# Attention scores with the keys as the streamed operand: rows of scores are copied out and turned, where keys were the stationary operand and gave columns of scores

## The chip, the cores and the metric

One core of a Trainium2 chip runs the whole program in one launch. The metric is device time in microseconds, from start to end of one execution; three runs of the kernel before gave 1105.93, 1108.88 and 1117.53, so the median is 1108.88. Engines are named as the profile names them: PE (TensorE matmul) and PEld (its weight loads), DVE (VectorE), ACT (ScalarE), POOL (GpSimd), SP (the queue that issues the DMAs).

## The reference

Eight rows with one token each (D = 448) go through two layers with the same weights. Each layer is attention over a cache of 4096 keys and values, then a small MLP block. With one token per row the shifted concatenation in the block contributes nothing, because every shift moves the only token out of the sequence:

```python
def _A_ref(x, k_cache, v_cache, wq, wo):        # B=8, Hq=16, Hkv=8, Sk=4096, Dh=256
    q = (x @ wq).reshape(B, 1, Hq, Dh).transpose(0, 2, 1, 3)
    k, v = jnp.repeat(k_cache, 2, axis=1), jnp.repeat(v_cache, 2, axis=1)
    p = softmax(einsum("bhqd,bhkd->bhqk", q, k) * Dh ** -0.5)
    return einsum("bhqk,bhkd->bhqd", p, v).reshape(B, 1, 4096) @ wo

for _ in range(2):
    x = x + _A_ref(layernorm(x), k_cache, v_cache, wq, wo)
    y = layernorm(x)
    x = x + y + gelu(layernorm(y) @ w3) @ w4
```

Keys and values are bf16, 2 MB each for one head of one row (a head here is one of the 8 pairs of K and V, which serves two query heads). 64 such heads are read in each layer. Both layers read the same cache, so a part of it can stay on the chip between a row's first and second layer.

## The kernel before, in words

**Tiles and slots.** A head's K or V is cut into four units of 512 KB ("quarters"); the tile `kv` has 30 slots of one unit each. Position m of 128 partitions holds 32 consecutive keys, 8 of them in each unit. For a row's heads 3 to 7 (`kept_heads`) most of K, and the last 6 units of V, stay in their slots from the first layer to the second; heads 0 to 2 (`free_heads`) are loaded anew in both. A load is issued as soon as a slot is given free, by the scores for K (`o.frees` in `front`) and by the PV products for V (in `back`). Neighbouring units whose slots lie together go in one DMA of up to 2 MB.

**One head, first half (`front`).** Each new K unit arrives with keys along the partitions. `transpose_piece` turns it on PE in pieces: two bf16 elements are taken as one fp32, four 128x128 transposes (L1219) fill a bank `psT` (four banks), and DVE (L1202) or ACT (L1203) copies it back over the unit in `kv`. After it the 256 dimensions of a key lie on 128 partitions, the even and the odd ones in alternate elements (`c`, a step of two). The scores of a unit (`sc`, L1037) are 16 matmuls: for 8 groups of 128 keys and both `c`, the turned keys are the 128 stationary columns, and the two query columns, repeated `REP` = 24 times, are the 48 streamed columns. A score lands with its key on a partition, two columns per group, in `psM[:, 256 + 2i]`. From these 64 columns per head follow the softmax steps: copy to `sS` (L1056), maximum (L1059, over the partitions on POOL L1061), `nb` (L1065), exponentials to `pT` (ACT L1071), their sum (POOL L1075).

**One head, second half (`back`).** PV (L1104): for each group of 128 keys the two columns of `pT` are stationary and 256 columns of V are streamed; four groups of keys use four column groups of the array (`tile_position=(0, 32 * (i % 4))`), so that four partial sums stand on partitions 0, 32, 64 and 96. DVE copies and splits them into two bf16 parts (L1118, L1120), four small matmuls with `sel` add them (L1128), and L1134 divides. Four matmuls (L1153) add the head's share of `x @ wo` to a row in `psR`; when 7 heads are in, two DVE steps (L1163, L1165) and ten matmuls turn that row (`turn`), and the last head is added by L979 and L982.

**Order.** The functions do not emit instructions. They record operations with their engine, a duration in microseconds, what they read and write, the PSUM banks they use, and a priority; the class `Plan` then lays them out in time and writes one fixed order per engine, with semaphores between them. An operation of kind "ev" goes to DVE or ACT, whichever the planner finds free. An operation that touches a bank waits for the last user of that bank on each other engine. The planner also puts `filler` matmuls (L1424: 248 columns into a `psP` bank, or 512 into a `psT` bank) where it thinks PE is idle and the recent number of streamed columns is low, to keep PE's clock up.

**Loops.** Row by row: the kept heads of a row's first layer, the free heads of the next row drawn into them (`both`); then `mid` (MLP, L725 to L982, and the second layer's queries, L817 with L1275); then the second layer's heads, kept ones first; weights are loaded once (L605).

Of the kernel before, what the change touches and what calls it, by code (L numbers as in the profile page):

```python
# [6 lines left out]
P = 128  # L7
B = 8
D = 448
# [15 lines left out]
REP = 24  # L25
# [16 lines left out]
PV1 = PV0 + DH  # L42
QW, HW, YW = 24, 24, 12
SC = 448
YC = 0

# [414 lines left out]
def bass_interleave_layers__gqa_block_cached__mixer_s_mlp__decode_kernel(  # L461
# [53 lines left out]
    xoT = sb("xoT", [P, NC5, B - 2], bf)  # L515
    acc = [sb(f"acc{i}", [P, NC5], f32) for i in range(2)]
    base = sb("base", [P, NC5, B], f32)
    mask = sb("mask", [P, NC5], bf)
    xc = sb("xc", [P, NC5, B], f32)
    mom = sb("mom", [P, 3, B], f32)  # L520
# [5 lines left out]
    t_h = sb("t_h", [P, 28], f32)  # L526
    var = sb("var", [P, 2, B], f32)
    rsi = sb("rsi", [P, 2, B], i32)
    rst = sb("rst", [P, 2, B], f32)
    rsy = sb("rsy", [P, 2, B], f32)  # L530
    yb = sb("yb", [P, NC5, B], bf)
# [3 lines left out]
    o_last = sb("o_last", [P, G], bf)  # L535
    q2T = [sb(f"q2T{i}", [P, 32], bf) for i in range(2)]
    cursor[0] = (cursor[0] + 31) // 32 * 32
    hb0 = cursor[0]
    hb = sb("hb", [P, 14 * B], bf)
    g1 = sb("g1", [P, 14 * B], f32)  # L540
    row0 = cursor[0] - 448
    g2 = sb("g2", [P, 14 * B], f32)
    hT = sb("hT", [P, 14 * B], bf)

    oW = nc.alloc_sbuf_tensor_at("oW", [P, 2 * D], bf, offset=hb0)
    cursor[0] = max(cursor[0], hb0 + 4 * D)

    x_row = nc.alloc_sbuf_tensor_at("x_row", [B, NC5 * P], bf, offset=row0)
    o_row = nc.alloc_sbuf_tensor_at("o_row", [B, D], bf, offset=row0)
    assert row0 + 2 * NC5 * P <= hb0 + 4 * D  # L550
# [11 lines left out]
    oS = sb("oS", [P, 2, DH], bf)  # L562
    sel = sb("sel", [P, 2], bf)
# [10 lines left out]
    psM, M, SB = nc.alloc_psum_tensor("psM", [P, 512], f32), "M", 256  # L574
# [33 lines left out]
    def dma_once(name, parts, keys, at):  # L608

        for i, (dst, src, nbytes, *row) in enumerate(parts):  # L610
            dma(name, dst, src, nbytes, nc.alloc_semaphore(f"s_{name}{i}"), 16, [keys[i]],
                4 * at - 0.5, *row)
# [27 lines left out]
    YB = ["yb"]  # L640

    def const_a(gp):
        gp.memset(ident_f[:, :], 0.0)
        gp.memset(x_row[:, D:D + P], 0.0)
        gp.memset(mask[:, :], 1.0)
        gp.memset(x3T[:, :, :], 0.0)
        for t, c in [(t, 1) for t in x1c + x2c] + [(xf, 2)]:
            gp.memset(t[:, :, c:c + 1], 1.0)
            last = gp.memset(t[:, :, c + 1:c + 2], -1.0)
        return last  # L650
    plan.op("pool", const_a, 1.0, "const", wr=["ident0", "xr2", "mask0", "one", "x3all"])
# [48 lines left out]
    def rsqrt(c, n):  # L700
# [6 lines left out]
        for half, three in RSQRT_STEPS:  # L707
            dv(lambda v: v.tensor_tensor(tt, yy, yy, ALU.mult), rd=["rsy"], wr=["rst"])
            dv(lambda v, half=half: v.scalar_tensor_tensor(tt, tt, -half, vv, ALU.mult, ALU.mult),
               rd=["rst", "var", "var1"], wr=["rst"])  # L710
# [46 lines left out]
    def norm(src, skey, second, B):  # L757
# [23 lines left out]
        if second:  # L781
# [4 lines left out]
           rd=["mom", skey], wr=["xc"])  # L786
# [3 lines left out]
           rd=["xc", "rsy"], wr=["yb"])  # L790
# [72 lines left out]
    def last_rows(src, skey, n, ps, bank):  # L863
# [28 lines left out]
        def yrow(t):  # L892
            last = None
            for fc in range(14):
                for g in range(4):
# [7 lines left out]
                                            ALU.add), 0.2, rd=["psM", "xs"], wr=["o_last"], banks=[bank])  # L903
# [5 lines left out]
    def mlp(src, skey, n, dst, dkeys):  # L909
# [6 lines left out]
        h_, a_, b_ = hb[:, 0:m], g1[:, 0:m], g2[:, 0:m]  # L916
        if few:
# [4 lines left out]
            for r in range(n):  # L922
                dv(lambda v, r=r: v.tensor_scalar(t_h[:, r * 14:(r + 1) * 14], cs_h[:, :], minus_mean(n, r),
                                                  rsy[:, 1, r:r + 1], ALU.mult, ALU.mult),
                   rd=["mom", "rsy", "cs_h"], wr=["t_h"] if r == 0 else [("t_h", r)])
# [7 lines left out]
        else:  # L933
# [7 lines left out]
           rd=HB, wr=["g1"])  # L941
        dv(lambda v: v.scalar_tensor_tensor(b_, a_, GELU_K, h_, ALU.add, ALU.mult),
           rd=HB + ["g1"], wr=["g2"])
        plan.op("act", lambda a: a.activation(a_, b_, ACT.Tanh), 0.3, "chain",
                rd=["g2"], wr=["g1"], prio=urge[0] + len(plan.ops))
# [49 lines left out]
    def front(layer, b, h, prio=None):  # L995
# [8 lines left out]
        if layer == 0:  # L1004
            def rhs(c):
                return q1T[:, b, 4 * h + 2 * c:4 * h + 2 * c + 2]
            qk = [("q1T", 0), ("q1T", 1)]
        else:
            def rhs(c):
                return q2T[b % 2][:, 4 * h + 2 * c:4 * h + 2 * c + 2]  # L1010
            qk = [("q2", b, h)]
# [10 lines left out]
        for u in range(4):  # L1022
# [6 lines left out]
            def sc(t, u=u, q=ks[u]):  # L1029
                last = None  # L1030
                for s in range(8):
                    i = 8 * u + s


                    for c in range(2):
                        a = slot_ap(q, s * 256, 256)
                        last = t.matmul(ps[:, SB + 2 * i:SB + 2 * i + 2 * REP], a[:, c:256:2],  # L1037
                                        bcast(rhs(c), REP, 1), start=(c == 0), stop=(c == 1))
                return last
            o = plan.op("pe", sc, (0.022 * 16 + 0.06, 32 * REP / 1200 + 0.01, 32 * REP, 16), "sc",  # L1040
                    rd=qk + [("s", ks[u], 0), ("s", ks[u], 1)],
                    wr=[("sc", par, x) for x in range(u, 4)], banks=[bk],
# [9 lines left out]
        hi = len(plan.ops) - 10 ** 5  # L1052
        scs = [("sc", par, x) for x in range(4)]
# [27 lines left out]
    def back(layer, b, h):  # L1081
# [15 lines left out]
        for u in range(4):  # L1097

            def pv(t, u=u, q=vs[u]):
                last = None  # L1100
                for s in range(8):
                    i = 8 * u + s
                    g4 = 32 * (i % 4)
                    last = t.matmul(ps[g4:g4 + 2, PV0:PV0 + DH], pT[nr][:, i, :],  # L1104
# [7 lines left out]
            if u == 0:  # L1112
                o.tbank = bk
# [10 lines left out]
        def sum_mm(t):  # L1124
# [12 lines left out]
            wr=[("oT", no)], banks=[bk], prio=hi).tbank = bk  # L1137
# [24 lines left out]
        if k == HKV - 1:  # L1162
            dv(lambda v: v.tensor_copy(oW[:, 0:D], psR[:, 0:D]), 0.55, rd=[kr],  # L1163
               wr=["hb", "g1", "g2", "hT"], banks=["R"], name="acc", prio=hi)
# [319 lines left out]
```

## Time and profile before

| | kernel before |
|---|---|
| median of three runs | 1108.88 us |
| the profiled execution: time, span of its instructions | 1107.5 us, 1105.7 us |
| mean granted PE clock | 0.927 |
| busy: PE, PEld | 970.7 us (88%), 775.8 us (70%) |
| busy: DVE, ACT, POOL | 572.6 us (52%), 287.7 us (26%), 97.6 us (9%) |
| DMA queue q1 | 438.41 MB in 54356 packets |
| L1037 scores (PE) | 8192 matmuls, 288.5 us busy |
| L1219 transposes (PE) | 2816 matmuls, 388.6 us busy |
| L1104 PV (PE) | 4096 matmuls, 187.5 us busy |
| L1202, L1203 (DVE, ACT): turned keys back to `kv` | 415 x 690 ns, 321 x 585 ns |
| L1424 fillers | 184 of 248 columns, 42 of 512 |

How to read it: a group's "mean" for a matmul is the time from its start to its modelled end, of which most is pipeline, so it says little about how fast matmuls follow one another; for that one compares the starts of successive runs of instructions in the timeline. The slices of the page are fortieths of the span, 27.6 us each. The DMA share is the busy share of 16 engines; over a short stretch it can stand slightly above 1, since a packet counts where it starts. "issue" is time in which an engine waited for nothing that the profile shows.

### The profile page before, as it was taken

Reading aid. Unit: us, or ns where it says so; the run is one execution under the profiler, and the core shown is the slowest. Engines: PE = TensorE matmul, PEld = TensorE weight load, DVE = VectorE, ACT = ScalarE, POOL = GpSimd, SP = SyncE. Lnnn points to the kernel's source line nnn. Section 1 sums busy time; section 2 is a strip of 40 time slices with the busy share of each in tenths; the row PEclk is TensorE's granted clock in tenths of the full one; section 3 lists DMA queues with packets and bytes.
Section 4 is the critical chain, followed back from the end, with each engine's and each line's share of the span. In section 5 each row is a group of like instructions: output and inputs, shape, how many; then the busy total and the mean of one; then the engine's idle time right before and its main releaser. Section 6 shows DMA issues by size and latency. Waiting matters only on the chain.

```text
span 1105.7 us, 42629 instructions
## 1 busy us (share of the span) xinstructions
PE 970.7 (88%) x19504; PEld 775.8 (70%) x19504; DVE 572.6 (52%) x1782; ACT 287.7 (26%) x844; POOL 97.6 (9%) x275
## 2 busy tenths in 40 slices
PE   4889889898899988998988898998889898899987
PEld 4668657785678856786666865778567785688674
DVE  4345445554455544655544554565545655356644
ACT  1133113331224302242122321233112331234120
POOL 0000010010100101010000100100010100101010
PEclk9899989998899979999888989999979999799998
DMA  9999999999999999999999999999999999999994
GB/s 333 406 426 420 391 392 424 424 421 388 400 422 425 419 355 426 423 424 420 368 424 426 419 359 358 423 425 416 393 396 424 424 404 388 413 416 398 360 408 178
DMA packets 54543, 441.13 MB, mean 399 GB/s; under 512 B 5838, under 2 KB 9052, under 8 KB 27100
## 3 DMA queue, kind: packets, MB, share of 16 engines
q1 hardware_dynamic: 54356, 438.41, 97.2%
q8 instruction: 153, 2.51, 0.9%
q14 instruction: 26, 0.21, 0.0%
q10 hardware_dynamic: 8, 0.00, 0.0%
HBM read 438.38 MB, written 0.01 MB: 396 GB/s over the span
## 4 chain that ended last, share of the span: by engine, by line
PE 56%; DMA 32%; SPq 4%; issue 4%; DVE 3%; ACT 1%; POOL 0%
PE psT L1219 20%; DMA kv<-in_A_k_cache_dram 19%; PE psM L1037 16%; DMA kv<-in_A_v_cache_dram 13%; PE psP L1104 9%; SPq L622 4%; PE psR L1153 4%; PE psM L817 2%; PE psP L1424 1%; PE psP L1128 1%; PE psM L979 1%; DVE oS L1120 1%; DVE oS L1118 1%; PE psM L982 1%; ACT pT L1071 1%
## 5 line engine op out<-in xcount | busy, mean ns | idle before, releaser
L1219 PE MATMUL psT<-ident_f,kv 128*128 128x128 f32 x2816 | 388.6, 284 | 24.0 <-DMA kv<-in_A_k_cache_dram 23.3
L1202 DVE COPY kv<-psT 128x512 f32<-128x512 f32 x415 | 284.1, 690 | 176.5 <-PE psT L1219 170.0
L1219 PEld LDWEIGHTS psT<-ident_f,kv 128*128 128x128 f32 x2816 | 312.0, 144 | 48.4 <-DMA kv<-in_A_k_cache_dram 28.8
L1203 ACT COPY kv<-psT 128x512 f32<-128x512 f32 x321 | 186.5, 585 | 386.1 <-PE psT L1219 385.4
L1104 PE MATMUL psP<-kv,pT 128*2 128x256 bf16 x4096 | 187.5, 293 | 30.7 <-issue 16.9
L1037 PEld LDWEIGHTS psM<-q2T,kv 128*128 128x128 bf16 x4096 | 129.9, 100 | 46.7 <-issue 34.8
L1037 PE MATMUL psM<-q2T,kv 128*128 128x48 bf16 x4096 | 145.3, 189 | 13.2 <-issue 10.8
L1037 PEld LDWEIGHTS psM<-q1T,kv 128*128 128x128 bf16 x4096 | 134.3, 97 | 17.5 <-issue 11.2
L1037 PE MATMUL psM<-q1T,kv 128*128 128x48 bf16 x4096 | 143.2, 184 | 1.1 <-issue 0.4
L1104 PEld LDWEIGHTS psP<-kv,pT 128*2 128x2 bf16 x4096 | 79.1, 84 | 72.0 <-issue 27.3
L1071 ACT ACTIVATE pT<-sS,nb,fac 128x32 bf16<-128x32 f32 x128 | 52.7, 417 | 242.5 <-DVE nb L1065 242.5
L1061 POOL PARTITION_ALL_REDUCE gm<-pm x128 | 45.5, 355 | 758.3 <-DVE pm L1059 710.2
L1056 DVE COPY sS<-psM 128x64 f32<-128x64 f32 x128 | 28.5, 223 | 107.9 <-PE psM L1037 105.2
L1118 DVE CAST oS<-psP 128x256 bf16<-128x256 f32 x128 | 53.9, 421 | 51.4 <-PE psP L1104 49.2
L1153 PE MATMUL psR<-wo_sb,oT 128*1 128x448 bf16 x448 | 68.7, 390 | 5.0 <-DVE oT L1134 2.0
L1075 POOL PARTITION_ALL_REDUCE Db<-rs x128 | 51.0, 398 | 215.6 <-ACT pT L1071 215.6
L1128 PE MATMUL psP<-sel,oS 128*128 128x2 bf16 x512 | 32.4, 167 | 33.0 <-DVE oS L1120 29.2
L1128 PEld LDWEIGHTS psP<-sel,oS 128*128 128x128 bf16 x512 | 25.4, 100 | 49.8 <-DVE oS L1120 41.4
L1071 ACT ACTIVATE pT<-sS,nb 128x32 bf16<-128x32 f32 x128 | 40.9, 326 | 68.7 <-DVE nb L1065 68.7
L1120 DVE TENSOR_TENSOR oS<-psP,oS 128x256 bf16<-128x256 f32 x128 | 54.1, 423 | 3.5
L817 PEld LDWEIGHTS psM<-x2c,wq_sb 128*128 128x128 bf16 x768 | 30.7, 98 | 18.5 <-DVE sS L1056 6.1
L817 PE MATMUL psM<-x2c,wq_sb 128*128 128x24 bf16 x768 | 36.6, 184 | 5.0 <-issue 4.3
(159 smaller groups left out, 574.5 us busy)
## 6 DMA issues: line engine op xcount, KB each, us to landing
kv<-in_A_k_cache_dram SPq DMA_DIRECT2D x72, 2048.0 KB, 20.1
kv<-in_A_v_cache_dram SPq DMA_DIRECT2D x54, 2048.0 KB, 17.6
kv<-in_A_v_cache_dram SPq DMA_DIRECT2D x125, 512.0 KB, 7.5
kv<-in_A_v_cache_dram SPq DMA_DIRECT2D x54, 1024.0 KB, 10.7
kv<-in_A_k_cache_dram SPq DMA_DIRECT2D x23, 1024.0 KB, 12.2
kv<-in_A_v_cache_dram SPq DMA_DIRECT2D x5, 1536.0 KB, 10.2
kv<-in_A_k_cache_dram SPq DMA_DIRECT2D x12, 512.0 KB, 7.6
wo_sb<-in_A_wo_dram SPq DMA_DIRECT2D x1, 3584.0 KB, 45.5
```

The source lines that it names most:

```text
L817: last = t.matmul(bank[:, at + i * step:at + i * step + copies], w, r, start=(kc == 0), stop=(kc == 3))
L1037: last = t.matmul(ps[:, SB + 2 * i:SB + 2 * i + 2 * REP], a[:, c:256:2], bcast(rhs(c), REP, 1), start=(c == 0), stop=(c == 1))
L1071: return a.activation(pT[nr][:, :, :].rearrange("p i j -> p j i")[:, jj, :], sview[:, jj, :], ACT.Exp, bias=nb[nm][:, jj:jj + 1], scale=sc ...
L1075: plan.op("pool", lambda gp: gp.partition_all_reduce(Db[nr][:, :], rs[nr][:, :], P, RO.add), 0.5, "sum", rd=[("rs", nr, 0), ("rs", nr, 1)] ...
L1104: last = t.matmul(ps[g4:g4 + 2, PV0:PV0 + DH], pT[nr][:, i, :], slot_ap(q, s * 256, 256), start=(i < 4), stop=(i >= 28), skip_group_check= ...
L1118: plan.op("dve", lambda v: v.tensor_copy(oS[:, 0, :], po), 0.36, "o", rd=[("pv", par, x) for x in range(4)], wr=["oS0"], banks=[bk], prio=hi)
L1120: plan.op("dve", lambda v: v.tensor_tensor(oS[:, 1, :], po, oS[:, 0, :], ALU.subtract), 0.36, "o", rd=["oS0"] + [("pv", par, x) for x in r ...
L1128: last = t.matmul(ps[:, PV1 + 2 * c:PV1 + 2 * c + 2], oS[:, w, c:DH:2], sel[:, :], start=(w == 0), stop=(w == 1))
L1153: last = t.matmul(psR[r:r + 1, 0:D], oT[no][:, i % 2, i // 2:i // 2 + 1], wo_sb[:, a:a + D], start=(k == 1 and i < 2), stop=(k == HKV - 1 ...
L1202: return e.tensor_copy(dst, psT[bank][:, :])
L1203: return e.copy(dst, psT[bank][:, :])
L1219: last = t.transpose(psT[bank][:, s * P:(s + 1) * P], src, ident_f[:, :])
```

## The change

**Scores.** The turned keys become the streamed operand and the queries the stationary one. A unit's 16 groups (8 groups of keys, two `c`) become 8 matmuls: for each `c` and each of four column groups, 256 keys are streamed, as every second element of 512, past four query columns. Of these four, two are the head's queries and two are zeros, in an order that depends on whether the unit's number is even or odd (`typ`); so an even and an odd unit add up in the same four PSUM rows per column group, and half a head (two units, `half`) stands as 4 rows x 256 columns on four groups of partitions in `psM[:, 128:384]`. For the padding the queries are kept in `q1b` and `q2T` with zeros on both sides; for the first layer POOL copies them from `q1T` once per row.

**Copy and turn.** The whole 128 x 256 block is copied to a single fp32 buffer `sR` by DVE or ACT, and two fp32 matmuls, with 128 columns of `sR` stationary and 16 columns of the fp32 identity streamed, write the scores back as columns into `psM[:, 64:128]`. The softmax steps then go on as before, with the keys of `pT` in another order, which PV's index follows.

**Fillers** go only to `psT` banks. **Room** in the on-chip memory for `sR` and the padded queries is made by letting tensors share memory (`xoT` with `x3T`, `xc` and `yb` with `g1`, `t_h` with `hT`, `x_row` with `w4_sb`, `o_last` with `oS`, the second GELU buffer with the first). For that, the row sum is split and turned in two parts, and the loads of `w4` wait until `x_row` has been read.

```diff
 def front(layer, b, h, prio=None):
     if layer == 0:
-        def rhs(c):
-            return q1T[:, b, 4 * h + 2 * c:4 * h + 2 * c + 2]
-        qk = [("q1T", 0), ("q1T", 1)]
+        if h == 0:
+            plan.op("pool", lambda gp: gp.tensor_copy(
+                q1b[b % 2][:, :, :, 2:4],
+                q1T[:, b, :].rearrange("p (h c j) -> p h c j", c=2, j=2)), 0.2, "chain",
+                rd=[("q1T", 0), ("q1T", 1), "q0"], wr=[("q1b", b % 2)])
+        qb = q1b[b % 2]
...
-            def sc(t, u=u, q=ks[u]):
-                for s in range(8):
-                    i = 8 * u + s
-                    for c in range(2):
-                        a = slot_ap(q, s * 256, 256)
-                        last = t.matmul(ps[:, SB + 2 * i:SB + 2 * i + 2 * REP], a[:, c:256:2],
-                                        bcast(rhs(c), REP, 1), start=(c == 0), stop=(c == 1))
-            o = plan.op("pe", sc, (0.022 * 16 + 0.06, 32 * REP / 1200 + 0.01, 32 * REP, 16), "sc",
+            typ, half = u % 2, u // 2
+            def sc(t, typ=typ, q=ks[u]):
+                for c in range(2):
+                    w = qb[:, h, c, 2 - 2 * typ:6 - 2 * typ]
+                    for g in range(4):
+                        last = t.matmul(ps[32 * g:32 * g + 4, SR:SR + DH], w,
+                                        slot_ap(q, g * 512, 512)[:, c:512:2],
+                                        start=(typ == 0 and c == 0), stop=(typ == 1 and c == 1),
+                                        skip_group_check=True, tile_position=(0, 32 * g))
+            o = plan.op("pe", sc, (0.25, 0.46, 512, 8), "scr",
...
+            if typ:
+                def out_rows(e):
+                    if e is nc.vector:
+                        return e.tensor_copy(sR[:, :], ps[:, SR:SR + DH])
+                    return e.copy(sR[:, :], ps[:, SR:SR + DH])
+                plan.op("ev", out_rows, {"dve": 0.42, "act": 0.4}, "evh", rd=[("sr", half)], wr=["sR"],
+                        banks=[bk], prio=hi)
+                def turn_s(t, half=half):
+                    pick = ident_f[:, :].rearrange("p (g r) -> p g r", g=4)[:, :, 0:4]
+                    for j in range(2):
+                        a = SB + 32 * half + 16 * j
+                        last = t.matmul(ps[:, a:a + 16], sR[:, j * P:(j + 1) * P], pick, start=True, stop=True)
+                plan.op("pe", turn_s, (0.3, 0.5, 128, 2), "ts", rd=["sR", "ident_f"], wr=[("st", par, half)],
+                        banks=[bk], prio=hi)
...
 def back(layer, b, h):
-                    last = t.matmul(ps[g4:g4 + 2, PV0:PV0 + DH], pT[nr][:, i, :],
+                    at = 16 * (u // 2) + 8 * (s % 2) + 2 * (s // 2) + u % 2
+                    last = t.matmul(ps[g4:g4 + 2, PV0:PV0 + DH], pT[nr][:, at, :],
...
-            dv(lambda v: v.tensor_copy(oW[:, 0:D], psR[:, 0:D]), 0.55, rd=[kr], ...)
-            dv(lambda v: v.tensor_tensor(oW[:, D:2 * D], psR[:, 0:D], oW[:, 0:D], ALU.subtract), ...)
+            for a, mts in [(0, range(2)), (2 * P, range(2, NC5))]:
+                w = min(2 * P, D - a)
+                dv(lambda v, a=a, w=w: v.tensor_copy(oW[:, 0, 0:w], psR[:, a:a + w]), 0.42, rd=[kr], ...)
+                dv(lambda v, a=a, w=w: v.tensor_tensor(oW[:, 1, 0:w], psR[:, a:a + w], oW[:, 0, 0:w],
+                                                       ALU.subtract), 0.42, ...)
...
 def filler(bank):
-        if bank in (0, 1, 2, 3):
-            dst, n = psT[bank][:, :], 512
-        else:
-            dst, n = psP[int(bank[1])][:, PV1 + 8:512], 248
+        dst, n = psT[bank][:, :], 512
```

## The prediction

> **What bounds the kernel now.** First the page's slices, to see which resource never rests (DMA share, GB/s moved, queues):
>
> ```profile
> DMA  9999999999999999999999999999999999999994
> GB/s 333 406 426 420 391 392 424 424 421 388 400 422 425 419 355 426 423 424 420 368 424 426 419 359 358 423 425 416 393 396 424 424 404 388 413 416 398 360 408 178
> q1 hardware_dynamic: 54356, 438.41, 97.2%
> q8 instruction: 153, 2.51, 0.9%
> ```
>
> The transfers fill every slice but the last. The best slices move 424 to 426 GB/s; 438.4 MB at 425 would take 1031.6 us of the 1105.7. So at most 74 us lie outside the transfers at full rate, and the change loads the same bytes. To see where, I asked for busy times by stage: a stretch in which keys are turned, one around the passage from a row's first layer to its second, and the end.
>
> ```profile
> core 0: us, PE busy (x) PEld busy (x) DVE busy (x) ACT busy (x) POOL busy (x), PEclk, DMA share, GB/s
> 180.00:260.00 80.00, 72.32 (x1297) 61.60 (x1295) 46.61 (x116) 27.38 (x78) 7.93 (x21) 0.98 1.01 422
> 260.00:300.00 40.00, 34.44 (x824) 24.00 (x825) 16.75 (x78) 4.80 (x19) 3.01 (x8) 0.79 0.98 380
> 1084.00:1106.00 22.00, 17.56 (x355) 9.63 (x346) 10.81 (x46) 0.23 (x1) 0.00 (x0) 0.83 0.28 111
> ```
>
> In the turning stretch the DMA share is 1.01, so DMA sets the pace, but PE is busy 72.3 of 80 us, a close second. At the passage the rate drops to 380 while the share is still 0.98: most of that loss is not idleness. Over 260:300, 400:440, 520:560 and 640:700 the shares are 0.98, 0.99, 0.98, 0.94, idle 0.8+0.4+0.8+3.6 = 5.6 us, so about 10 us over all seven passages. The end has 22 us with hardly a transfer. Third, the chain of waits, and one stop in the timeline near the end:
>
> ```profile
> PE 56%; DMA 32%; SPq 4%; issue 4%; DVE 3%; ACT 1%; POOL 0%
> ```
> ```profile
> 1083.38 0.38 PE L1104 MATMUL psP<-kv,pT 128*2 128x256 bf16 x5 [2.75 <-issue]
> ```
>
> PE carries over half of that chain, and 4% (44 us) is "issue", in which PE waited for nothing that is shown. The prices come from the groups, and from starts in the timeline, because a matmul's own duration contains its pipeline:
>
> ```profile
> L1219 PE MATMUL psT<-ident_f,kv 128*128 128x128 f32 x2816 | 388.6, 284 | 24.0 <-DMA kv<-in_A_k_cache_dram 23.3
> L1104 PE MATMUL psP<-kv,pT 128*2 128x256 bf16 x4096 | 187.5, 293 | 30.7 <-issue 16.9
> L1037 PE MATMUL psM<-q2T,kv 128*128 128x48 bf16 x4096 | 145.3, 189 | 13.2 <-issue 10.8
> L1037 PE MATMUL psM<-q1T,kv 128*128 128x48 bf16 x4096 | 143.2, 184 | 1.1 <-issue 0.4
> L1118 DVE CAST oS<-psP 128x256 bf16<-128x256 f32 x128 | 53.9, 421 | 51.4 <-PE psP L1104 49.2
> ```
> ```profile
> 606.35 1.07 PE L1219 MATMUL psT<-ident_f,kv 128*128 128x128 f32 x8
> 607.26 0.56 PE L1037 MATMUL psM<-q1T,kv 128*128 128x48 bf16 x16
> 607.67 0.64 PE L1219 MATMUL psT<-ident_f,kv 128*128 128x128 f32 x4
> ...
> 615.30 0.56 PE L1037 MATMUL psM<-q1T,kv 128*128 128x48 bf16 x16
> 615.79 0.62 PE L1104 MATMUL psP<-kv,pT 128*2 128x256 bf16 x16
> 616.34 0.57 PE L1037 MATMUL psM<-q1T,kv 128*128 128x48 bf16 x16
> ```
> ```profile
> 261.06 1.04 PE L1104 MATMUL psP<-kv,pT 128*2 128x256 bf16 x32 [0.35 <-DMA kv<-in_A_v_cache_dram]
> 262.03 0.40 PE L1424 MATMUL psP<-ident_f 128*128 128x248 bf16 x2
> ```
>
> **The scores.** A unit (a quarter of a head's keys) costs 16 matmuls: 607.26 to 607.67, 0.41 us. The new form is shaped like L1104: few weight columns, 256 columns streamed, four column groups. There 32 take 0.97 us, so 8 take 0.24. Between full-array work the groups cost entry and exit: the score before PV takes 0.49 instead of 0.41, and 16 PV take 0.55 instead of 0.485, so 0.15 per round trip. A lone unit comes to 0.24 + 0.15 = 0.39 (saving 0.02), a pair to 0.63 against 0.82 (0.09 each). The order of the changed program has both, so I take 0.05: 512 x 0.05 = 26 us. Upper end: the busy means, 288.5/512 - 187.5/512 = 0.20, or 101 us. Lower end: no row streams with a step of two elements; at half rate a unit costs 0.24 more, a loss of 0.22 to 0.15.
>
> The Trainium skill, "TensorEngine Tiling (Array Packing)", section Tiling Modes, says that changing the tiling mode drains TensorE, which speaks against scattering column groups among transposes. The 0.15 above is what that costs here; by its other claim alone, up to 4x for four column tiles, the switch would seem free of it.
>
> **The turn.** Two fp32 matmuls per half head, 512 in all: 128 columns of fp32 weights, 16 columns streamed. No row shows a true fp32 product; the nearest is L1219, an fp32 transpose, 0.91/8 = 0.114 us each and bound by its weights. One such pass: 0.23 per turn, 58 us. Four: 0.91, 233 us. I take two, 0.46 per turn, 117 us, since the built program holds two pairs of weight load and matmul for each of these 512 instructions.
>
> The skill's "FP8 and Floating Point Precision", section TensorE Precision Notes, says that true fp32 takes four passes through the array. Four passes that each reload weights would give the 233 us.
>
> **The copy between.** 256 copies of 128x256 fp32, 0.42 us by L1118 (half of L1202's 690 is 0.345): 108 us, 173 of them on DVE, 83 on ACT. DVE is busy 46.6 of 80 us and ACT 27.4 in the turning stretch; 16 copies add 6.7 between them, so both stay far from full. Queued behind a late copy are transpose evictions (L1202, L1203), for which PE waited 0.2 us in all: cover. The wait that is added is PE's: the turn stands in PE's order after the copy, and PV, transposes and the output row queue behind it. Copy and hand-overs need 0.57 us. In the changed order 210 of the 256 turns have at least 0.5 us of other PE work before them (two transpose groups 0.9, 16 PV 0.55), the other 46 less than 0.3, 16 of these none. Exposed: 20 us over the run if DVE is at once free, 50 if it is 0.3 late. I take 20, or 0.16 per head.
>
> **PE's sum where it matters.** 80 us of the turning stretch hold 422 x 80 / 4194 = 8 heads. Per head: 2 x 0.46 + 0.16 - 4 x 0.05 = +0.88, for 8 heads 7.0 us. Idle are 7.7, and 2.8 more are fillers (L1424 in that stretch). 7.0 of 10.5: DMA keeps the bound, with 3.5 us to spare.
>
> **The passages.** Per kept head the second layer issues 64+32+16+4+4 = 120 pairs; after it 32+32+16+4+4 and 8 for the turns, 96. Fewer pairs, fewer "issue" stops: a fifth of 44 us would be 9, mostly under transfers; I count 3 at the end, where 2.75 stands before a backlog of PV. Instruction traffic falls by the 16% of all pairs, 0.9% x 1106 x 0.16 = 1.6 us of the DMA engines. Against it, the first score row of the second layer becomes weights later by copy, turn and hand-overs, 0.42 + 0.46 + 0.2 = 1.1 us, so the kept V slots are refilled later: with transfers drained there, 8 x 1.1 = 9. Key slots are freed by the scores themselves, not by the turn.
>
> **At nothing:** the padded copy of the queries (8 on POOL, busy 9%, under the first K load; 0.2 us each otherwise); the split row sum, 4 x 0.42 for 2 x 0.62 on DVE, before the last head's V lands; w4's loads, behind the first row's transposes in SP's queue, done some 80 us before; shared buffers, whose last readers are a stage back; 141 fillers of 512 columns for 184 of 248 and 42 of 512, only into idle PE.
>
> **Sum.** 9 - 3 - 1.6 = +4. The profiled execution took 1107.5 (span 1105.7), so 1112; the median 1108.9 is 1.4 higher: 1113.
>
> **Rivals.** *PE tips over (slower):* each turn costs four passes. Per head 2 x 0.91 + 0.16 - 0.2 = 1.78, for 8 heads 14.2, 3.7 beyond the 10.5; over some 750 us of such stretches 35 on top: 1148. It decides from a turn of 0.68 us. For it: only the price of an fp32 weight pass is shown. Against: two pairs. *The strided stream runs at half rate:* 1.08 + 4 x 0.19 = 1.84, 14.7 for 8, 4.2 beyond, 39 on top: 1152. For: no such row. Against: L1037's weights have that step and load in 100 ns, L979's, without it, in 96. *The feed recovers (faster):* with fewer pairs, PE frees slots in time at the passages (10 idle), the end loses its stop (3) and the fetches shrink (2): -15, 1094. Against: "issue" stops lie under a DMA share of 1.
>
> **Chances.** About 1% (11 us) is what a measurement here can tell from no change. Likeliest 0.50, its range 1102 to 1124 (same 0.35, slower 0.15); four passes 0.15; stride 0.10; recovered feed 0.25 (faster 0.20, same 0.05). Faster 0.20, same 0.40, slower 0.40. Range 1090 to 1152.
>
> **What would show it.** The turn's starts 0.46 apart from the next work, against 0.9; eight score matmuls in 0.24; a DMA share of 1 and 420 GB/s in turning stretches, with PE at 76 of 80; passages no emptier than 0.94. Wrong would be a rate below 410 in the turning stretches, or a PE clock under 0.9 there (0.98 now).

## The result, and the profile after

| | before | after |
|---|---|---|
| median of four runs each | 1110.53 us (1105.93 to 1117.53) | 1128.95 us (1121.61 to 1134.6) |
| ratio to before, 95% interval | | 1.0162 [1.0124, 1.0200] |
| profiled execution: time, span | 1107.5, 1105.7 us | 1121.6, 1119.7 us |
| mean granted PE clock | 0.927 | 0.887 |

The changed kernel is 1.6% slower. The range of the prediction, 1090 to 1152, holds its time; the likeliest case, 1113 us, is 16 us short, and the time lies above that case's own range, 1102 to 1124. The profiled execution is the fastest of its four, so the traces show 14 of the 18 us between the medians. Below, medians and ratios leave out the executions that stand more than 1.5% above the fastest of the same kernel (two of four in e10_no_fill, one of four in e6_double).

From the page of the changed kernel: busy times, transfer share and GB/s of the 40 slices, the queues and the chain of waits.

```profile
PE 1032.3 (92%) x16347; PEld 753.7 (67%) x16347; DVE 630.4 (56%) x1964; ACT 333.1 (30%) x950; POOL 99.7 (9%) x287
...
DMA  9999999999999999999999999999999999999793
GB/s 347 409 425 418 384 403 425 424 422 330 404 426 426 402 338 407 424 425 401 364 416 425 404 389 380 425 425 416 387 399 426 424 398 380 410 420 384 283 395 152
...
q1 hardware_dynamic: 54932, 438.41, 96.7%
q8 instruction: 128, 2.10, 0.7%
...
PE 79%; DVE 8%; DMA 8%; issue 2%; ACT 1%; POOL 0%; POOLq 0%
```

The bytes are the same and the good slices still move 424 to 426 GB/s, but the chain has gone over to PE: 79% of it instead of 56%, and DMA 8% instead of 32%. "issue" has halved. The queue's packets took 0.967 x 1119.7 = 1083 us, before 0.972 x 1105.7 = 1075; what neither q1 nor q8 fills grew from 21 to 29 us. So some 8 us are time in which the transfer engines had nothing of these queues, and 8 us are packets that took longer, less 2 of instruction traffic.

The windows, with columns as in the prediction (busy us of PE, PEld, DVE, ACT, POOL, then clock, DMA share, GB/s): first one passage of the kernel before, then the changed kernel's turning stretches, passages and end:

```profile
400.00:440.00 40.00, 34.58 (x786) 25.60 (x787) 17.02 (x69) 6.99 (x26) 3.76 (x10) 0.83 0.99 391
```
```profile
180.00:260.00 80.00, 75.61 (x1053) 56.53 (x1049) 48.17 (x125) 32.03 (x88) 8.24 (x23) 1.00 1.00 417
260.00:300.00 40.00, 35.31 (x651) 22.07 (x655) 18.38 (x81) 4.54 (x17) 2.26 (x6) 0.67 0.96 356
400.00:440.00 40.00, 37.14 (x653) 25.15 (x646) 20.68 (x83) 5.80 (x19) 2.26 (x6) 0.67 0.99 373
560.00:640.00 80.00, 78.56 (x1210) 59.28 (x1211) 46.02 (x134) 31.96 (x90) 9.03 (x24) 0.98 1.00 415
700.00:780.00 80.00, 78.81 (x1188) 60.64 (x1187) 51.79 (x138) 32.47 (x90) 8.28 (x22) 1.00 1.01 424
...
1098.00:1120.00 22.00, 15.21 (x299) 8.23 (x297) 10.60 (x47) 1.13 (x5) 0.70 (x2) 0.84 0.19 75
```

In the turning stretches PE is at 75.6 to 78.8 of 80 us, and the transfers still run at 415 to 424 GB/s with a share of 1.00: they pace these stretches as before. Two passages move less: 380 to 356 and 391 to 373 GB/s, where the clock also fell from 0.79 and 0.83 to 0.67. Windows at fixed times are a weak witness, though: 640:700 moves more than before (387 for 365), and the run e1 below, no slower than the kernel before, has 351 at 260:300. To see where the time comes from, the two traces are laid side by side by the number of megabytes that have been loaded, worked out from the packets of all queues:

```
MB loaded      0-100  100-110  110-150  150-180  180-200  200-230  230-250
after-before    -1.1     +3.1     +0.1     +3.5     -0.2     +2.1     +0.1  us
MB loaded    250-290  290-360  360-400  400-410  410-430  430-440  the end
after-before    -2.4      0.0     +1.5     -0.7     +7.2      0.0     +0.8  us   sum +14.0
```

Nothing is lost over 110-150, 180-200, 230-250 and 290-360 MB, where the turning stretches lie: 0.0 us in all. The steps lie at passages, half of the sum at 410-430 MB (in the trace of before about 1010 to 1064 us). Not every passage loses: 290-360 MB holds the one at 780:820, and 250-290 MB the one at 640:700. Against e1, which has the same order and the time of the kernel before, the changed kernel loses 4.1 us at 150-180 MB, 2.5 at 200-230, 3.0 at 250-290 and 6.1 at 410-430, and nothing at 100-110; so the 3.1 us there do not come from the turn's price. Each of these is one execution against one, and executions of the changed kernel differ by up to 13 us, so a single step of 2 or 3 us says little. The chain of waits at the largest step, 1010:1062, by line, before and after:

```profile
by line: DMA kv<-in_A_v_cache_dram 33.6%; PE psT L1219 20.4%; PE psM L1037 15.5%; PE psP L1104 9.1%; PE psM L817 5.6%; PE psM L979 3.6%; PE psM L982 2.9%; PE psR L1153 2.5%; ACT pT L1071 1.8%; issue 1.7%; PE psP L1424 1.1%; PE psP L1128 0.9
```
```profile
by line: PE psT L1248 30.8%; PE psM L1045 12.2%; PE psP L1132 10.6%; PE psM L1076 10.0%; PE psM L823 3.9%; PE psM L985 3.7%; PE psR L1179 3.3%; ACT pT L1098 3.2%; PE psM L988 2.5%; DVE oS L1146 2.4%; DVE oS L1144 2.3%; issue 2.2%; ACT sR L1
```

And within the passage 400:440, again before and after:

```profile
by line: PE psM L1037 27.1%; DMA kv<-in_A_v_cache_dram 19.5%; PE psP L1104 15.6%; issue 9.9%; PE psT L1219 9.2%; PE psR L1153 7.6%; PE psM L817 7.3%; PE psP L1128 1.2%; DVE oS L1118 1.1%; DVE oS L1120 1.1%; DVE sS L1056 0.6%; PE psP L1424 0
```
```profile
by line: DMA kv<-in_A_v_cache_dram 18.5%; PE psP L1132 17.3%; PE psM L1076 14.6%; PE psM L1045 11.9%; PE psT L1248 8.7%; PE psR L1179 4.1%; PE psM L839 4.0%; PE psM L823 3.7%; ACT pT L1098 2.3%; DVE oS L1144 2.1%; PE psT L1452 2.1%; DVE oS
```

At the largest step the transfers of V held a third of the chain before and are no longer among its larger parts after; PE's work has taken their place, the turn (L1076) with 10.0%. At 400:440 the turn has 14.6%, 5.8 of 40 us, but there the scores have given up as much: 27.1% before, 11.9 + 14.6 = 26.5% with the turn after. Next the costliest groups of the changed kernel that the change touches, with busy time, mean of one, idle before it:

```profile
L1248 PE MATMUL psT<-ident_f,kv 128*128 128x128 f32 x2816 | 394.8, 282 | 1.0 <-DMA kv<-in_A_k_cache_dram 0.8
L1132 PE MATMUL psP<-kv,pT 128*2 128x256 bf16 x4096 | 193.9, 308 | 8.7 <-DMA kv<-in_A_v_cache_dram 5.2
L1076 PEld LDWEIGHTS psM<-ident_f,sR 128*128 128x128 f32 x1024 | 146.5, 206 | 52.7 <-DVE sR L1066 39.1
L1076 PE MATMUL psM<-ident_f,sR 128*128 128x16 f32 x1024 | 157.2, 268 | 15.9 <-DVE sR L1066 11.9
L1066 DVE COPY sR<-psM 128x256 f32<-128x256 f32 x173 | 73.3, 424 | 138.9 <-PE psM L1045 138.0
L1045 PE MATMUL psM<-kv,q2T 128*4 128x256 bf16 x2048 | 110.2, 312 | 3.2 <-DVE q2T L1304 2.8
L1045 PE MATMUL psM<-kv,q1b 128*4 128x256 bf16 x2048 | 96.6, 279 | 0.1
```

The first line says much: PE's idle time for a K unit has gone from 24.0 us to 1.0. When PE comes to a unit of keys, it is nearly always there already: PE runs behind the feed now. Scores went from 288.5 to 206.8 us busy (L1045, both lines), and the turn took 157.2. And the timeline of PE in a turning stretch, start and length in us:

```profile
605.71 0.63 PE L1045 MATMUL psM<-kv,q1b 128*4 128x256 bf16 x16
606.27 1.09 PE L1248 MATMUL psT<-ident_f,kv 128*128 128x128 f32 x8
607.20 0.52 PE L1076 MATMUL psM<-ident_f,sR 128*128 128x16 f32 x4
607.56 0.63 PE L1248 MATMUL psT<-ident_f,kv 128*128 128x128 f32 x4
608.12 0.41 PE L1045 MATMUL psM<-kv,q1b 128*4 128x256 bf16 x8
608.46 1.09 PE L1248 MATMUL psT<-ident_f,kv 128*128 128x128 f32 x8
```

A lone unit of scores takes 0.34 us (608.12 to 608.46), a pair 0.56 (605.71 to 606.27), and this turn 0.36 with its four pairs of weight load and matmul.

### The profile page after: what moved, and what is told of

Its sections match the earlier page's. It is cut to its first block, busy times and chain, and to the rows that moved or that the text cites. A ratio compares the mean times of both kernels' runs of the same rounds, so it can differ in the third digit from the quotient of the medians.

```text
span 1119.7 us, 36483 instructions
## 1 busy us (share of the span) xinstructions
PE 1032.3 (92%) x16347; PEld 753.7 (67%) x16347; DVE 630.4 (56%) x1964; ACT 333.1 (30%) x950; POOL 99.7 (9%) x287
## 4 chain that ended last, share of the span: by engine, by line
PE 79%; DVE 8%; DMA 8%; issue 2%; ACT 1%; POOL 0%; POOLq 0%
PE psT L1248 31%; PE psM L1045 13%; PE psP L1132 10%; PE psM L1076 10%; DMA kv<-in_A_v_cache_dram 5%; PE psR L1179 4%; DMA kv<-in_A_k_cache_dram 3%; PE psM L823 3%; PE psT L1452 3%; DVE sR L1066 2%; DVE oS L1146 2%; DVE oS L1144 1%; PE psM L985 1%; PE psP L1154 1%; ACT pT L1098 1%
## 5 line engine op out<-in xcount | busy, mean ns | idle before, releaser
L1231 DVE COPY kv<-psT 128x512 f32<-128x512 f32 x392 | 268.6, 690 | 149.7 <-PE psT L1248 134.6
L1232 ACT COPY kv<-psT 128x512 f32<-128x512 f32 x344 | 200.6, 586 | 333.3 <-PE psT L1248 333.1
L1076 PEld LDWEIGHTS psM<-ident_f,sR 128*128 128x128 f32 x1024 | 146.5, 206 | 52.7 <-DVE sR L1066 39.1
L1076 PE MATMUL psM<-ident_f,sR 128*128 128x16 f32 x1024 | 157.2, 268 | 15.9 <-DVE sR L1066 11.9
L1066 DVE COPY sR<-psM 128x256 f32<-128x256 f32 x173 | 73.3, 424 | 138.9 <-PE psM L1045 138.0
L1132 PEld LDWEIGHTS psP<-kv,pT 128*2 128x2 bf16 x4096 | 93.7, 88 | 52.6 <-ACT pT L1098 12.9
L1045 PE MATMUL psM<-kv,q2T 128*4 128x256 bf16 x2048 | 110.2, 312 | 3.2 <-DVE q2T L1304 2.8
L1098 ACT ACTIVATE pT<-sS,nb,fac 128x32 bf16<-128x32 f32 x128 | 52.7, 417 | 169.0 <-DVE nb L1092 169.0
L1045 PE MATMUL psM<-kv,q1b 128*4 128x256 bf16 x2048 | 96.6, 279 | 0.1
L1045 PEld LDWEIGHTS psM<-kv,q2T 128*4 128x4 bf16 x2048 | 47.3, 89 | 28.9 <-issue 8.0
L1067 ACT COPY sR<-psM 128x256 f32<-128x256 f32 x83 | 30.9, 372 | 99.0 <-PE psM L1045 98.8
```

The lines of the kernel that those rows point to most:

```text
L1045: last = t.matmul(ps[32 * g:32 * g + 4, SR:SR + DH], w, slot_ap(q, g * 512, 512)[:, c:512:2], start=(typ == 0 and c == 0), stop=(typ == 1 ...
L1066: return e.tensor_copy(sR[:, :], ps[:, SR:SR + DH])
L1076: last = t.matmul(ps[:, a:a + 16], sR[:, j * P:(j + 1) * P], pick, start=True, stop=True)
L1098: return a.activation(pT[nr][:, :, :].rearrange("p i j -> p j i")[:, jj, :], sview[:, jj, :], ACT.Exp, bias=nb[nm][:, jj:jj + 1], scale=sc ...
L1132: last = t.matmul(ps[g4:g4 + 2, PV0:PV0 + DH], pT[nr][:, at, :], slot_ap(q, s * 256, 256), start=(i < 4), stop=(i >= 28), skip_group_check ...
L1231: return e.tensor_copy(dst, psT[bank][:, :])
```

## The experiments

Theory A: the fp32 turn makes PE the bound. Against it: B, the colder clock at the passages costs the time; C, the planner was told 0.3 us for a turn and so laid out a bad order; D, not PE's work but the turn's latency, in the chain from the scores to the weights, is what counts. Ratios are to the kernel before, with 95% intervals.

### The turn without fp32, in the same order (e1_bf_same)

```diff
+    sR_b = sR[:, :].bitcast(bf)[:, 1:2 * DH:2]
...
-    pick = ident_f[:, :].rearrange("p (g r) -> p g r", g=4)[:, :, 0:4]
+    pick = ident_b.rearrange("p (g r) -> p g r", g=4)[:, :, 0:4]
...
-    last = t.matmul(ps[:, a:a + 16], sR[:, j * P:(j + 1) * P], pick, start=True, stop=True)
+    last = t.matmul(ps[:, a:a + 16], sR_b[:, j * P:(j + 1) * P], pick, start=True, stop=True)
```

> The changed kernel in the same order on every engine, but the two matmuls of a turn read the upper 16 bits of the fp32 block as bf16 (scores are cut to bf16), so that each is one bf16 weight load and product in place of two fp32 ones. Theory A (the price of the fp32 turn makes PE the bound in the turning stretches): 256 turns cost some 0.45 us less each, about 110 us of PE, so PE waits for keys again and the time comes back to 1100 to 1112. Theory B (the colder clock at the passages, 0.67 against 0.80, is the cause): the clock stays as cold, the time stays within 5 us of the changed kernel, about 1125. Theory C (the planner was told 0.3 us for a turn, so its order is wrong): little gain either, since the order is the same, though the order then errs by less; 1115 to 1125.

1106.94 us, ratio 0.9952 [0.9931, 0.9973]; PE busy 948.8 us, 83.5 less than in the changed kernel. Its groups, and then its page's chain of waits:

```profile
L1249 PE MATMUL psT<-ident_f,kv 128*128 128x128 f32 x2816 | 398.7, 287 | 36.0 <-DMA kv<-in_A_k_cache_dram 35.8
L1077 PE MATMUL psM<-ident_f,sR 128*128 128x16 bf16 x512 | 52.3, 174 | 16.9 <-DVE sR L1067 13.3 <-ACT sR L1068 1.9
```
```profile
PE 48%; DMA 43%; DVE 5%; issue 2%; ACT 1%; POOL 0%; SPq 0%; POOLq 0%
```

The turn has 512 pairs instead of 1024 and 52.3 us instead of 157.2; PE waits for K again (36.0 us), and the transfers have 43% of the chain again (8% in the changed kernel, 32% before). PE's wait for the copy is as long as in the changed kernel (16.9 us for 15.9), and the mean clock is the same 0.887. So the copy, its wait, the rows form of the scores, the shared memory and the clock of this order are not what costs by themselves: the fp32 turn is. B as the only cause is refuted; whether the clock makes the fp32 turn dearer is looked at under e12. The bf16 turn is shorter as well as cheaper, so e1 does not part A from D. This is also the one complete form that is faster than the kernel before, by 0.5%, at the price that it cuts the scores to bf16.

### Half of the price, and double (e5_half, e6_double)

```diff
 e5_half
+    last = t.matmul(ps[:, a:a + 16], (sR_b if j else sR)[:, j * P:(j + 1) * P], pick_b if j else pick, ...)
 e6_double
-    for j in range(2):
+    for j in (0, 1, 0, 1):
```

> The changed kernel in the same order; of the two matmuls of a turn the first stays fp32 and the second reads the upper 16 bits as bf16. PE is spared about half of what the first run spared it, some 42 of 84 us busy. Theory A with a threshold (PE's work is covered by the transfers up to a point and counts in full beyond it): most of the gain is back already, 1107 to 1114. A without a threshold (every us of PE counts alike): halfway, 1115 to 1119.

> The changed kernel in the same order; each fp32 turn is made twice, with the same result, 512 more fp32 matmuls, some 110 us more of PE. Theory A with a threshold: PE is the bound nearly throughout, so at least 70 us of it count: 1195 to 1240. A without a threshold: another 20 us or so, 1145 to 1155. Theory B (colder clock at the passages): more work on PE keeps it warmer, 1120 to 1140.

Half: 1108.89 us, 0.9979 [0.9955, 1.0003], where A with a threshold had put it. Double: 1241.62 us, 1.1155 [1.1097, 1.1213], just above what A with a threshold had said, and far from A without one and from B. From the page of e6_double, its slices:

```profile
DMA  9998999978998899989989799996899979998792
GB/s 347 411 424 336 356 395 424 402 284 313 412 424 337 307 344 371 426 319 342 343 357 420 297 350 350 424 420 273 341 363 415 425 270 338 388 384 337 261 390 104
```

Even with twice the price there are slices at 420 to 426 GB/s between others at 270 to 340: the feed does not slow down evenly, it breaks off in parts of each row. Ordered by PE's busy time, with e12 from below, the runs of one and the same order give:

| | e1 | e5 | e12 | after | e6 |
|---|---|---|---|---|---|
| PE busy, us | 949 | 981 | 993 | 1032 | 1154 |
| ratio | 0.9952 | 0.9979 | 1.0036 | 1.0162 | 1.1155 |

From e1 to e5 a microsecond of PE costs about 0.1 us of time, from e5 to e12 0.5 and from there to the changed kernel 0.4, beyond it 0.9. In this series PE's work is hidden by the transfers up to about 980 us and not beyond.

### Where the price is paid (e12_kept_bf)

```diff
+    lhs = sR
+    if layer == 1 and h in kept_heads:
+        pick, lhs = ident_b.rearrange("p (g r) -> p g r", g=4)[:, :, 0:4], sR_b
...
-    last = t.matmul(ps[:, a:a + 16], sR[:, j * P:(j + 1) * P], pick, start=True, stop=True)
+    last = t.matmul(ps[:, a:a + 16], lhs[:, j * P:(j + 1) * P], pick, start=True, stop=True)
```

> The changed kernel with its own order, but the turn of the second layer's kept heads (40 of the 128 heads, 80 of the 256 turns) reads the upper 16 bits of the copied scores, so that these turns cost one bf16 pair per matmul instead of two fp32 pairs; all other turns stay fp32 (those 40 heads' scores are cut to bf16 on the way). These heads load little, and are where PE and not the transfers should set the pace. Theory A without a place (a microsecond of PE costs the same wherever it stands): 80 of 256 turns take 26 of the 83 us of PE time that e1 took, PE busy about 1006; between e5 (981, ratio 0.998) and the changed kernel (1032, 1.016) that is a ratio of about 1.007. Theory A with its place (the price is paid at the passages and the kept heads, the turning stretches have room): back to e1 and e5, 0.995 to 1.001. If the price is paid in the turning stretches instead, nearly nothing comes back: 1.012 to 1.016.

1112.64 us, 1.0036 [1.0010, 1.0062]. Windows of this run, the stretches and two passages:

```profile
180.00:260.00 80.00, 75.16 (x1047) 56.41 (x1043) 48.44 (x127) 31.78 (x87) 8.13 (x22) 1.00 1.00 421
400.00:440.00 40.00, 34.49 (x705) 22.15 (x698) 22.86 (x91) 7.48 (x25) 3.37 (x9) 0.78 1.01 395
520.00:560.00 40.00, 30.24 (x606) 17.39 (x594) 19.50 (x82) 4.44 (x17) 2.47 (x7) 0.71 1.00 386
560.00:640.00 80.00, 78.56 (x1186) 59.70 (x1183) 48.05 (x133) 34.30 (x91) 8.36 (x23) 1.00 1.00 420
700.00:780.00 80.00, 78.18 (x1146) 59.71 (x1145) 50.76 (x132) 31.75 (x88) 8.28 (x22) 0.98 1.00 420
```

The stretches are as full as in the changed kernel (75.2, 78.6, 78.2 of 80) and run at 420 GB/s, and yet some 60% of the loss against e1 is back (1.26 of 2.10 points), with 31% of the turns made cheap. That the price is paid in the stretches is refuted. The rates of two other passages have not come back, though: 356 GB/s at 260:300 and 373 at 780:820, with 356 and 379 in the changed kernel and 351 and 379 in e1. By megabytes loaded this run regains 3.9 us on the changed kernel at 150-180 MB, 2.3 at 200-230, 1.7 at 250-290 and 4.7 at 410-430, the places of the loss, and gives back 2.9 at 360-400. The chain within the passage 400:440 of this run:

```profile
by line: DMA kv<-in_A_k_cache_dram 44.9%; DMA kv<-in_A_v_cache_dram 16.0%; PE psP L1136 9.8%; PE psM L1046 5.8%; PE psM L986 3.4%; PE psM L824 3.3%; PE psT L1252 3.3%; PE psR L1183 3.1%; PE psM L989 2.8%; ACT pT L1102 2.3%; issue 1.2%; PE p
```

The turn is gone from its larger parts, and transfers hold 44.9 + 16.0% of it, where the changed kernel had 18.5% for V. The full return (0.995 to 1.001) did not come either. PE's busy time fell by 39 us, not the expected 26: these 80 turns weigh 0.49 us each, the other 176 only (83.5 - 39) / 176 = 0.25. With 39 instead of 26, the table's rate without regard to place would give about 1.002, inside the interval. So the kept heads carry more than their share because their turns take more of PE's time, not shown to be because a microsecond costs more there. The trace of the changed kernel shows why they take more: from start to next start (gaps over 0.4 us counted as 0.4) these 80 turns took 0.66 us each, at a granted clock of 0.83 on average, and the other 176 took 0.48 at 0.99. So the colder clock of the passages is part of the price of the fp32 turn there, though e1 with a clock nearly as cold (0.62 to 0.79) is as fast as the kernel before.

### Fillers and the clock (e2_psp_fill, e8_bf_psp, e10_no_fill, e11_bf_no_fill)

```diff
 e2_psp_fill, and with e1's edit e8_bf_psp
+    if bank in (0, 1, 2, 3):
+        dst, n = psT[bank][:, :], 512
+    else:
+        dst, n = psP[int(bank[1])][:, PV1 + 8:512], 248
 e10_no_fill, and with e1's edit e11_bf_no_fill
-    plan.filler = filler
```

> The changed kernel with the fillers of 248 columns into psP banks put back as before (392 of them and 65 of 512). Theory A: no gain, since fillers don't make the turn cheaper; the same or some us slower, 1123 to 1133. Theory B: the clock at the passages returns towards 0.80 and at least half of the 18 us is regained: 1110 to 1119. Theory C: no change, 1123 to 1133.

> The bf16 turn of the first run together with the fillers into psP banks. In the first run the clock at the passages is 0.62 to 0.79; with PE no longer the bound, warmer passages could free slots sooner: 1098 to 1105 if the clock counts there, 1105 to 1112 if transfers or the chain of dependent steps set the passages.

> The changed kernel without any fillers (141 fewer matmuls of 512 columns, 47 us busy). Occupancy counts: since PE is the bound where they stand late, some of it is regained, 1112 to 1124. Rival D: no gain, 1125 to 1132. Theory B (clock): colder passages, 1130 or more.

> The bf16 turn without any fillers. Occupancy counts only beyond the cover, and here PE is covered: no gain, 1104 to 1109; if the clock counts where PE is covered, 1110 or more.

| | median us | ratio | clock |
|---|---|---|---|
| fp32 turn, more fillers (e2) | 1129.99 | 1.0166 [1.0113, 1.0219] | 0.948 |
| fp32 turn (after) | 1128.95 | 1.0162 [1.0124, 1.0200] | 0.887 |
| fp32 turn, none (e10) | 1133.15 | 1.0204 [1.0153, 1.0255] | 0.868 |
| bf16 turn, more fillers (e8) | 1112.41 | 1.0000 [0.9975, 1.0025] | 0.934 |
| bf16 turn (e1) | 1106.94 | 0.9952 [0.9931, 0.9973] | 0.887 |
| bf16 turn, none (e11) | 1115.69 | 1.0035 [1.0010, 1.0060] | 0.858 |

More fillers and a clock of 0.948 bring nothing (e2), and with the bf16 turn they cost 0.5% (e8); leaving the fillers out of `psP` was not the mistake. This is not a test of the clock alone: e2's fillers are busy 92.0 us against 46.9, and PE as a whole is as busy as in the changed kernel (1032.4 us), so what the warmer clock saved on other work went into the fillers. Without any fillers e1 loses 0.8% and comes to 1115.69 us; 1110 or more had been given as the sign that the clock counts. With the fp32 turn 1133.15 us is past the 1130 given for that, but the loss of 0.4% lies within the intervals and comes from two executions only. What the clock is worth by itself stays open.

### The planner's prices (e3_true_dur, e4_bf_plan)

```diff
 e3_true_dur
-    plan.op("pe", turn_s, (0.3, 0.5, 128, 2), "ts", ...
+    plan.op("pe", turn_s, (0.5, 0.95, 128, 4), "ts", ...
 e4_bf_plan: e1's edit and
+    plan.op("pe", turn_s, (0.12, 0.2, 32, 2), "ts", ...
```

> The changed kernel with the planner told what a turn takes by the trace (0.5 us warm, 0.95 cold, 4 pairs of weight load and product in place of 0.3, 0.5 and 2). Theory A: no change beyond 4 us. Theory B: no change beyond 4 us, unless the number of fillers (78 for 141) makes the clock colder still. Theory C: regains most of the 18 us: 1110 to 1115.

> The bf16 turn of the first run with the planner told its price (0.12 us warm, 0.2 cold), so that order and fillers (209 of 512 columns) follow. Theory A: 1095 to 1110, at or below the kernel before, since PE has then less to do than before the change. Theory B: about 1120. Theory C: some us below the first run, whose order still assumes 0.3.

1127.42 us, 1.0137 [1.0096, 1.0177], which the intervals do not separate from the changed kernel; and 1110.82 us, 0.9994 [0.9969, 1.0018], not better than e1 with its order for 0.3 us. Theory C had put e3 at 1110 to 1115 and e4 below e1; it falls: an order made for the true price doesn't win the time back.

### No turn at all (e7_scores_only)

```diff
-            if typ:
-                def out_rows(e):
...
-        scs = [("st", par, x) for x in range(2)]
+        scs = [("sr", x) for x in range(2)]
```

> Copy and turn are left out, the scores stay as rows in PSUM and the softmax reads columns that nothing writes; order and fillers are planned anew. It shows what the new form of the scores earns by itself, without its price. If PE's load still counts in the first run: below it by 5 us or more, 1085 to 1100. If the transfers alone set the pace there: within 4 us of the first run, 1102 to 1110; then no cheaper turn can gain more.

1105.91 us, 0.9955 [0.9934, 0.9977], PE busy 934.3. One of its windows:

```profile
560.00:640.00 80.00, 70.57 (x934) 47.71 (x934) 40.98 (x102) 27.02 (x69) 6.41 (x17) 0.98 1.01 424
```

With neither copy nor turn it is no faster than e1: the transfers have a share of 1.01 in this stretch, and a turn cheaper than e1's would gain nothing. The whole saving at the scores is worth 5 us of time, though PE is busy 36 us less than in the kernel before (970.7).

### The same PE time elsewhere (e9_moved)

```diff
 e1's edit, and ahead of the output row's four matmuls of each head
+    for i in range(4):
+        t.matmul(ps[:, PV1 + 16:PV1 + 32], ident_f[:, :], ident_f[:, 0:16], start=False,
+                 stop=False, skip_group_check=True)
```

> The first run's bf16 turn in the same order, and 448 idle fp32 matmuls (four ahead of each output row's four, their result is not used) that give PE nearly the load of the fp32 turn at a place that no score waits for. Theory A in its form 'PE's occupancy counts, wherever it stands': back up to 1120 to 1130. Rival D, 'the turn's latency in the chain from scores to weights counts': the chain stays short, so 1106 to 1113.

1188.24 us, 1.0713 [1.0642, 1.0785]: far slower than any theory said. The added group, and two passages:

```profile
L1178 PE MATMUL psP<-ident_f 128*128 128x16 f32 x896 | 138.7, 289 | 3.1 <-DVE oT L1161 2.9
```
```profile
260.00:300.00 40.00, 34.81 (x603) 22.44 (x597) 17.68 (x77) 4.35 (x17) 2.26 (x6) 0.66 0.87 313
400.00:440.00 40.00, 34.77 (x561) 22.82 (x561) 17.96 (x74) 4.07 (x14) 1.72 (x5) 0.59 0.90 312
```

Here the chain from scores to weights has the cheap turn, so latency in that chain (D) isn't needed for a loss: fp32 work on PE is enough. Whether D has a share in the changed kernel's own loss no run shows, since every run that made the turn cheaper also made it shorter. But 138.7 us of it cost 81 us over e1, where the changed kernel pays 22 for 105 more (157.2 - 52.3). It stands between a head's `oT` and its share of the row, which the passage waits for, and the passages are the emptiest seen (313 GB/s, shares of 0.87 and 0.90). PE is also busier here, 1087.8 us, and the table's slopes would put some 70 us over e1 at that figure, so that much of the 81 may be amount and not place. The run can't tell the two apart.

## Why the prediction was right or wrong, point by point

**The number.** +4 us was said and +18 came. Slower had been given a chance of 0.40, no more than the same. The range holds the time because of its upper ends, 1148 and 1152, which stand for two rivals that did not come true; the likeliest case alone would have missed by 5 us. That the range held is luck more than insight.

**The bound, and "DMA keeps the bound, with 3.5 us to spare".** Right where it was worked out: in the turning stretches the share stays 1.00 and the rate above 410, PE at 75.6 to 78.8 where 76 was said, with 2.3 to 4.3 us of it fillers. By the megabytes, no time was lost there.

**The passages: the step that failed.** "Sum +4" prices the turn there by one late score row for each row's second layer; the traces show +14 instead, at passages. PE's sum per head was made for the turning stretch alone, where the transfers hide it. The passages are where the second layer's kept heads stand (in the changed kernel's trace every score between 265 and 300 us reads `q2T`), which load little and bring two turns each: 40 heads, 80 turns. No price was put on these. The traces show the loss at passages, the chain there has the turn in it, and e12 gets 60% of the gap to e1 back by cheapening these 80 turns, which take 52 of the turn's 137 us. Their weight was in reach: 40 x 0.88, by the prediction's own figure, is 35 us of PE where the transfers cover little, as an upper bound. Whether the 9 us for the late row came as reckoned is not separated.

**The scores.** Mis-sized, to the good: 0.05 us per unit was said and 0.16 measured, (288.5 - 206.8) / 512; from the starts of successive matmuls (gaps over 0.4 us counted as 0.4) it is the same, 249 less 168 us. In the timeline above a lone unit saves 0.07 (0.34 for 0.41) and a pair 0.26 (0.56 for 0.82), against 0.02 and 0.19. So a round trip between full-array work and column groups cost 0.07 to 0.10 us (0.34 or 0.56 less 0.24 or 0.485), not 0.15. The rest was not expected: the old scores cost 0.487 by starts, not 0.41, with the waits among them. The strided stream is not slower: by starts 41 ns for one of its matmuls beside 43 for one of PV. The rival at half rate is refuted.

**The turn.** Two pairs, as counted. The median from one pair's start to the next is 112 ns at a high clock, so 0.45 per turn, as said (0.46). At a low clock it is 214 ns, 0.86; over the run 137 us by starts, 0.54 per turn, against 117 and 0.46. The Trainium skill's four passes ("FP8 and Floating Point Precision", section TensorE Precision Notes) would have given an estimated 0.91 if each reloaded the weights; the trace shows two instruction pairs and half that price at a high clock, and how many passes a pair makes inside is not visible.

**The copy and its wait.** 173 copies of 424 ns and 83 of 372, as priced. PE's matmuls at L1076 waited 15.9 us and its weight loads 52.7, against 20 to 50. They are not what made the kernel slower: e1 has the same waits (16.9 and 53.8) and is fast.

**"Issue" and instruction traffic.** q8 fell from 2.51 to 2.10 MB, the 16% that was said. The chain's "issue" fell from 4% to 2%, but the 3 us at the end were not gained: from the 440th megabyte on, the changed kernel takes 0.8 us longer.

**The clock** was to fall under 0.9 in the stretches if the forecast was wrong. It is 0.98 to 1.00 there, and 0.66 to 0.74 at the passages, where nothing had been forecast.

**The rivals.** "PE tips over" had the right engine, but at four passes a turn and in the stretches, and neither came. Its deciding point of 0.68 us per turn is too high: 0.54 already tips, a turn with one fp32 matmul of two (e5) does not. It got its point from the room in the stretches, and so missed the passages. "The feed recovers" is refuted: the passages lost time, and the end gained none.

## What to carry to other kernels

In this kernel a PE saving and a PE cost were worth next to nothing while the transfers paced the stretch, and most of their price where PE carried the chain: make the sum for each stage, above all for the one that loads little, and not from the mean slack. Here 82 us less at the scores bought 5 us, and a 105 us dearer turn cost 22. When turning data on PE, see first whether its precision allows a form in bf16; the small matmul with fp32 weights was dear by its two weight loads, with 112 ns from pair to pair for 16 streamed columns where the transposes take 109 for 128.

## What the runs showed of the hardware

- A matmul with 128x128 fp32 weights and 16 streamed columns is two pairs of weight load and matmul: 0.22 us at the full granted clock and 0.43 at half of it, where the bf16 one of the same shape has a median of 39 ns to the next start at the full clock.
- A bf16 stream of every second element, past four stationary columns in four column groups, runs as fast as a contiguous one past two: over the run 41 and 43 ns from start to next start for one matmul of 256 columns.
- Filler matmuls raised the mean granted clock from 0.887 to 0.948 and changed the time by nothing that can be measured (1.0162 and 1.0166), since they took as much of PE as the clock gave back; taking the last fillers away cost e1 0.8%, with the clock at 0.858.
